# Issuing one attention tile and one output chunk ahead, and moving small elementwise steps between engines

## The chip, the cores and the metric

The kernel runs on one core of one Trainium2 chip. The metric is the device time in microseconds (us) of one execution; lower is better. TensorE is called PE here, VectorE DVE, ScalarE ACT, GpSimd POOL, and SyncE, whose queue issues nearly all the DMAs, SP. PEld is PE's weight load.

## The reference

One block of a network over 2048 tokens of width 448, in bf16. A vector c gives six modulation vectors (`silu(c) @ w_mod`). First half: layer norm, scale and shift, attention with 16 heads of width 28 in its linear form, projection by `wo`, gated residual. The feature map of a head is a softmax of `q @ w_phi` joined with a softmax of its negative (the same for k). Second half: layer norm, scale and shift, a gated MLP that mixes along the tokens, gated residual.

```python
# attention, per head: phi(u) = concat(softmax(u w_phi), softmax(-u w_phi))
kv  = phi(k)^T v                 # summed over all 2048 tokens
z   = sum over tokens of phi(k)
o   = (phi(q) kv) / (phi(q) z + 1e-6)
x   = x + ga * (o @ wo)
# gated MLP
zz  = gelu(h @ w_in)             # 448 -> 1792
z1, z2 = first 896, layernorm(last 896)
g   = w_sp @ z2 + b_sp           # 2048 x 2048 over the tokens
x   = x + gb * ((z1 * g) @ w_out)
```

## The kernel before, in words

The program is written for a planner. The Python code issues operations in some order, which counts as their priority; the planner sorts each engine's queue before the run, taking what is ready by its own reckoning, earlier-issued work first, and adds the semaphores. At run time every engine takes its queue strictly in order. Tiles of one tag share a fixed number of buffers (`bufs`), so an operation can also wait for a buffer.

Tokens are worked in 16 tiles of 128, and in four super-tiles of 512 tokens (four tiles each).

- **First stage (A1).** For each tile: k and v (lines 235, 236) in PSUM, `softmax_feats` (lines 196 to 209) on k, the sums over features and their reciprocal on DVE (239, 240), the scaled features `phik` on POOL (242), and the accumulation of `kvacc` on PE (249). `softmax_feats` takes the maximum and minimum of each head on DVE (200, 201), subtracts the maximum (203, DVE), forms minimum minus maximum, 16 numbers a token (204, DVE), forms the negated half from it (205, POOL), and takes the exponential on ACT (208).
- **Late setup.** `late_setup` (253) folds the gates into the weights: `g_rep` holds two gate rows on all partitions in float32 (266), `wo_s` is multiplied by the first (267, 268), the seven slices of `wout_s` by the second (270).
- **Second stage (A2).** For each super-tile `st`: `a2_q` on its four tiles (307: q, `softmax_feats`, a transposing DMA to `EqT`), then for each tile `il` first `a2_o` (316) and then, of the super-tile before, `a2_z2` (352) and a share of `a2_z1` (371). `a2_o` is the whole attention output of a tile: eight matmuls `num` (321), two reciprocals and two multiplies on DVE (326, 327), the sum `tt` and `rden` on POOL (329, 331), a reciprocal and the scaling `o_rot` on DVE (332, 334), a transposing DMA to `oT` (337), the projection with the residual `x1_ps` on PE (341, 342), layer norm through DVE and POOL (185 to 191), `xn2` on ACT (346) and four transposes into `tp` on PE (348). After the fourth tile ACT makes `h2T` from `tp` (396), on which `a2_z2` and `a2_z1` of this super-tile then work during the next. A fifth pass has only that last work. The two `num` halves share two PSUM banks, `x1_ps` and `z2_ps` share two (tag `xz`), `q_ps` and `z1_ps` share two (tag `qz`).
- **Last stage (B).** For each of four chunks of 512 tokens, and each of seven feature slices: 16 matmuls of 512 columns into `g_ps` (426), the bias on DVE (428), the product with `z1T` on POOL (429). When the seven are done, the chunk's four output tiles: seven matmuls over the slices (434), an eighth with the identity that adds the residual `x_sb` (435), a copy to bf16 on ACT (437), and the store (438). The weights of the next chunk are loaded by four transposing DMAs on SP (69).

Of the kernel before, what the change touches and what calls it, by code (L numbers as in the profile page):

```python
# [9 lines left out]
ALU = mybir.AluOpType  # L10
AX = mybir.AxisListType
BF = mybir.dt.bfloat16
F32 = mybir.dt.float32
PSUM = bass.MemoryType.PSUM

P = 128
D = 448
# [3 lines left out]
KC = 4  # L21
FH = 896
FC = 7
# [5 lines left out]
def kernel(  # L29
# [14 lines left out]
    dbg=None,  # L44
# [49 lines left out]
    g_rep = sl.tile([P, 2, D], F32, name="g_rep")  # L94
# [101 lines left out]
    def softmax_feats(pool, p_ps, tagp):  # L196
# [7 lines left out]
        nc.vector.tensor_tensor(out=mn[:], in0=mn[:], in1=mx[:], op=ALU.subtract)  # L204
# [48 lines left out]
    def late_setup():  # L253
# [13 lines left out]
        nc.vector.tensor_tensor(out=wo_s[:, 0:3, :], in0=wo_s[:, 0:3, :], in1=g_rep[:, 0:1, :].to_broadcast([P, 3, D]), op=ALU.mult)  # L267
        nc.vector.tensor_tensor(out=wo_s[0:64, 3, :], in0=wo_s[0:64, 3, :], in1=g_rep[0:64, 0, :], op=ALU.mult)
# [47 lines left out]
    def a2_o(i, il, EqT, tp):  # L316
# [20 lines left out]
        nc.sync.dma_start_transpose(out=oT[:], in_=o_pad[:])  # L337
        x1_ps = psA.tile([P, D], F32, name="x1_ps", tag="xz")
# [10 lines left out]
        if dbg is not None and "o" in dbg:  # L349
            nc.sync.dma_start(out=dbg["o"][i * P:(i + 1) * P, :], in_=o_pad[:, 0:D])  # L350
# [27 lines left out]
    prev = None  # L378
    for st in range(NST + 1):
# [3 lines left out]
        for il in range(4):  # L383
            if st < NST:
                a2_o(st * 4 + il, il, EqTs[il], tp)
            if prev is not None:
                pst, ph2T = prev
                a2_z2(pst * 4 + il, il, ph2T)
                for fc in range(*z1_split[il]):
                    a2_z1(pst, fc, ph2T)  # L390
            if st == 0:
                load_wsp_piece(wsp_tiles[0], 0, il) if False else None
        if st < NST:
            h2T = wk.tile([DC, KC, 512], BF, tag="h2T")
            for cc in range(KC):
                nc.scalar.activation(out=h2T[:, cc, :], in_=tp[:, cc, :], func=ACT.Identity,  # L396
                                     scale=colf[:, 12 + cc:13 + cc], bias=colf[:, 8 + cc:9 + cc])
            prev = (st, h2T)
    if dbg is not None:
# [14 lines left out]
    outv = out[0].rearrange("(n p) d -> n p d", p=P)  # L414
    for tcn in range(NTCH):
# [5 lines left out]
        wspT = wsp_tiles[tcn]  # L421
        tsl = slice(tcn * TCH, (tcn + 1) * TCH)
        for fc in range(FC):
            g_ps = psg.tile([P, TCH], F32, name="g_ps", tag="g")
            for sc_ in range(NT):
                nc.tensor.matmul(g_ps[:], lhsT=z2n[:, sc_, fc * P:(fc + 1) * P], rhs=wspT[:, sc_, :], start=(sc_ == 0), stop=(sc_ == NT - 1))  # L426
            gb_ = wk.tile([P, TCH], F32, tag="gb")
            nc.vector.tensor_tensor(out=gb_[:], in0=g_ps[:], in1=bsp[:, tsl], op=ALU.add)
            nc.gpsimd.tensor_tensor(out=z1T[:, fc, tsl], in0=gb_[:], in1=z1T[:, fc, tsl], op=ALU.mult)  # L429
        for tl in range(TCH // P):  # L430
            t = tcn * (TCH // P) + tl
            o_ps = pso.tile([P, D], F32, name="o_ps", tag="o")
            for fc in range(FC):
                nc.tensor.matmul(o_ps[:], lhsT=z1T[:, fc, t * P:(t + 1) * P], rhs=wout_s[:, fc, :], start=(fc == 0), stop=False)  # L434
            nc.tensor.matmul(o_ps[:], lhsT=ident[:], rhs=x_sb[:, t, :], start=False, stop=True)  # L435
            ot = wk.tile([P, D], BF, tag="ot")
            nc.scalar.copy(out=ot[:], in_=o_ps[:])  # L437
            nc.sync.dma_start(out=outv[t], in_=ot[:])
# [38 lines left out]
```

## Time and profile before

| what | value |
|---|---|
| median of 4 runs | 418.79 us (417.73 to 421.11) |
| the profiled execution | 417.73 us |
| its span in the profile | 415.9 us |
| mean granted PE clock | 0.852 of full speed |
| busy: PE, DVE, ACT, POOL | 318.1, 203.8, 152.6, 146.6 us |

The span is the part that the profiler saw; 1.8 us of the execution lie around it. Busy times are of the whole span, and the stages differ: PE is busy nearly all of the last stage, and no engine all of the others. Times in the rows further down are microseconds from the start of the span.

### The profile page before, as it was taken

How to read it: one execution, taken by the hardware profiler on the slowest of the kernel's cores; microseconds unless marked ns; L12 is line 12 of the kernel's file. 1: busy time of each engine (PE TensorE's matmuls, PEld its weight loads, DVE VectorE, ACT ScalarE, POOL GpSimd, SP SyncE). 2: the span in 40 equal slices, each digit the busy share in tenths (PEclk: the TensorE clock that was granted, in tenths of full speed). 3: DMA queues.
4: the chain of work that ended last, by engine and by line, in shares of the span. 5: the costliest groups of instructions: out<-in, count | busy, mean ns of one | idle time of the engine just before them, and what ended most of it. 6: DMA issues, size and time to landing. Idle time of an engine off the chain costs nothing.

```text
span 415.9 us, 4540 instructions
## 1 busy us (share of the span) xinstructions
PE 318.1 (76%) x1609; PEld 150.7 (36%) x1620; DVE 203.8 (49%) x471; ACT 152.6 (37%) x229; POOL 146.6 (35%) x198
## 2 busy tenths in 40 slices
PE   1668778544866869676686676499999999999995
PEld 1644334223322233323232232134444444444442
DVE  1478988874487865667456755235110110110110
ACT  1167827442130465559463955164002002002002
POOL 2035677772034543335223522112331331331331
PEclk9999868765556669966896699669999999999999
DMA  8999100000032241032203220000991008401001
GB/s 218 302 302 196 34 1 1 2 0 0 2 72 54 50 90 25 0 64 41 50 0 63 40 52 0 13 2 7 189 209 44 2 0 181 67 0 46 0 0 44
DMA packets 69071, 25.60 MB, mean 62 GB/s; under 512 B 59897, under 2 KB 68474, under 8 KB 69050
## 3 DMA queue, kind: packets, MB, share of 16 engines
q1 hardware_dynamic: 68082, 24.50, 28.2%
q10 hardware_dynamic: 968, 0.83, 0.9%
q8 instruction: 12, 0.20, 0.2%
q14 instruction: 9, 0.07, 0.1%
HBM read 8.81 MB, written 1.84 MB: 26 GB/s over the span
## 4 chain that ended last, share of the span: by engine, by line
PE 46%; DVE 19%; POOL 14%; ACT 8%; DMA 6%; issue 5%; SPq 1%; POOLq 0%; ACTq 0%; DVEq 0%
PE g_ps L426 23%; PE z_ps L357 4%; PE o_ps L434 4%; POOL phik L242 4%; PE x_ps L341 3%; POOL tt L329 3%; DVE sums L239 3%; PE z_ps L374 3%; DVE t L327 3%; POOL d L205 2%; DMA Wp<-in_A_wqkv_dram 2%; DMA wo_s<-in_A_wo_dram 2%; POOL rstd L189 2%; ACT xn L346 2%; ACT E_rot L208 2%
## 5 line engine op out<-in xcount | busy, mean ns | idle before, releaser
L426 PE MATMUL g_ps<-wspn,z2n 128*128 128x512 bf16 x328 | 72.6, 379 | 0.4
L426 PEld LDWEIGHTS <-z2n 128*128 128x128 bf16 x448 | 43.8, 98 | 53.6 <-issue 1.0
L437 ACT CAST ot<-o_ps 128x448 bf16<-128x448 f32 x16 | 8.5, 532 | 117.0 <-PE o_ps L435 115.4
L205 POOL TENSOR_TENSOR d<-mn,d 128x448 f32<-128x448 f32 x32 | 30.0, 942 | 37.5 <-DVE mn L204 37.4
L208 ACT ACTIVATE E_rot<-d 128x896 bf16<-128x896 f32 x32 | 30.1, 952 | 32.6 <-POOL d L205 32.6
L357 PE MATMUL z_ps<-win_sb,h2T 112*128 112x448 bf16 x128 | 33.9, 393 | 6.2 <-ACT z2g L359 5.1
L374 PE MATMUL z_ps<-h2T,win_sb 112*128 112x512 bf16 x112 | 35.3, 432 | 0.4 <-ACT h2T L396 0.4
L242 POOL TENSOR_TENSOR phik<-E_rot,sums 128x1024 bf16<-128x1024 bf16 x16 | 30.4, 1917 | 14.1 <-DVE sums L240 12.6
L310 PE MATMUL q_ps<-Wp,hT 112*128 112x448 bf16 x64 | 22.1, 483 | 11.0 <-DVE d L203 10.3
L341 PE MATMUL x_ps<-wo_s,oT 128*128 128x448 bf16 x64 | 23.9, 479 | 8.5 <-DMA oT<-o_rot 8.5
L434 PE MATMUL o_ps<-wout_s,z1T 128*128 128x448 bf16 x112 | 24.5, 353 | 3.1 <-POOL z1T L429 3.1
L188 POOL TENSOR_SCALAR rstd<-mv 128x1 f32<-128x1 f32 (+1 forms) x20 | 4.5, 223 | 63.0 <-DVE mv L186 55.2
L236 PE MATMUL v_ps<-Wp,hT 112*128 112x448 bf16 x64 | 22.6, 459 | 4.4 <-ACT vaug_rot L244 4.4
L321 PE MATMUL num<-KVbd,EqT 128*128 128x120 bf16 x128 | 15.6, 270 | 13.0 <-DVE t L327 9.3
L362 DVE BATCH_NORM_STATS2 stats<-z2g 128x6 f32<-128x448 bf16 x32 | 19.5, 621 | 11.7 <-ACT z2g L359 11.5
L329 POOL TENSOR_TENSOR tt<-t 128x464 f32<-128x464 f32 x16 | 16.4, 1024 | 24.6 <-DVE t L327 24.6
L426 PE MATMUL g_ps<-wsp,z2n 128*128 128x512 bf16 x109 | 24.2, 379 | 0.8 <-ACT z1T L375 0.7
L235 PE MATMUL k_ps<-Wp,hT 112*128 112x448 bf16 x64 | 21.7, 439 | 1.7 <-ACT hT L227 1.6
L357 PEld LDWEIGHTS <-h2T 112*128 112x128 bf16 x128 | 13.6, 107 | 22.0 <-issue 13.1
L359 ACT ACTIVATE z2g<-z_ps 128x448 bf16<-128x448 f32 x32 | 17.3, 544 | 9.0 <-PE z_ps L357 8.7
L239 DVE TENSOR_REDUCE sums<-E_rot 128x32 f32<-128x896 bf16 x16 | 16.9, 1067 | 7.5 <-ACT E_rot L208 7.5
L327 DVE TENSOR_TENSOR t<-num,rS 128x464 f32<-128x464 f32 x32 | 19.8, 628 | 0.3
(155 smaller groups left out, 496.0 us busy)
## 6 DMA issues: line engine op xcount, KB each, us to landing
x_sb<-in_A_x_dram SPq DMA_DIRECT2D x4, 448.0 KB, 5.7
out_dram<-ot SPq DMA_DIRECT2D x16, 112.0 KB, 1.7
win_sb<-in_B_w_in_dram SPq DMA_DIRECT2D x1, 1568.0 KB, 15.3
wmod_c<-in_w_mod_dram ACTq DMA_DIRECT2D x1, 784.0 KB
wmod_c<-in_w_mod_dram SPq DMA_DIRECT2D x1, 784.0 KB, 8.4
wmod_g<-in_w_mod_dram SPq DMA_DIRECT2D x2, 392.0 KB
wout_s<-in_B_w_out_dram SPq DMA_DIRECT2D x1, 784.0 KB, 16.7
bsp<-in_B_b_sp_dram SPq DMA_DIRECT2D x1, 512.0 KB
```

Of the source, the lines that this page charges most:

```text
L205: nc.gpsimd.tensor_tensor(out=d[:, :, 1, :], in0=mn[:].unsqueeze(2).to_broadcast([P, H, DH]), in1=d[:, :, 0, :], op=ALU.subtract)
L208: nc.scalar.activation(out=E[:, :, :, 0:DH], in_=d[:], func=ACT.Exp)
L236: nc.tensor.matmul(v_ps[:], lhsT=lhs, rhs=Wp[:, kc, 2 * D:3 * D], start=(kc == 0), stop=(kc == KC - 1))
L239: nc.vector.tensor_reduce(out=sums[:], in_=Ek[:, :, :, 0:DH], axis=AX.X, op=ALU.add)
L242: nc.gpsimd.tensor_tensor(out=phik[:], in0=Ek[:], in1=sums[:].unsqueeze(3).to_broadcast([P, H, 2, 32]), op=ALU.mult)
L327: nc.vector.tensor_tensor(out=t12[:, b], in0=numv[:, :, :, 0:29], in1=rS[:, b].unsqueeze(3).to_broadcast([P, 8, 2, 29]), op=ALU.mult)
L329: nc.gpsimd.tensor_tensor(out=tt[:], in0=t12[:, :, :, 0, :], in1=t12[:, :, :, 1, :], op=ALU.add)
L341: nc.tensor.matmul(x1_ps[:], lhsT=oT[0:kk, cc, :], rhs=wo_s[0:kk, cc, :], start=(cc == 0), stop=False)
L357: nc.tensor.matmul(z2_ps[:], lhsT=h2T[:, kc, il * P:(il + 1) * P], rhs=win_sb[:, kc, FH + hf * D:FH + (hf + 1) * D], start=(kc == 0), stop ...
L374: nc.tensor.matmul(z1_ps[:], lhsT=win_sb[:, kc, fc * P:(fc + 1) * P], rhs=h2T[:, kc, :], start=(kc == 0), stop=(kc == KC - 1))
L426: nc.tensor.matmul(g_ps[:], lhsT=z2n[:, sc_, fc * P:(fc + 1) * P], rhs=wspT[:, sc_, :], start=(sc_ == 0), stop=(sc_ == NT - 1))
L434: nc.tensor.matmul(o_ps[:], lhsT=z1T[:, fc, t * P:(t + 1) * P], rhs=wout_s[:, fc, :], start=(fc == 0), stop=False)
```

## The change

`a2_o` is cut in two after the `oT` transfer: `a2_o1` (from `num` to `oT`) and `a2_o2` (from the projection to the transposes). `a2_o1` of the next tile of the super-tile is now issued ahead of `a2_o2` of this tile and of the MLP work beside it. In the last stage the first feature slice of a chunk is issued ahead of the output tiles of the chunk before; the eighth matmul is gone, and the residual is added by DVE as it empties the PSUM bank, in place of ACT's copy. In `softmax_feats`, in both its uses, the small subtraction goes from DVE to POOL. `g_rep` is bf16, and `wo_s` is multiplied in four slices instead of two pieces.

```diff
-    g_rep = sl.tile([P, 2, D], F32, name="g_rep")
+    g_rep = sl.tile([P, 2, D], BF, name="g_rep")
...
-        nc.vector.tensor_tensor(out=mn[:], in0=mn[:], in1=mx[:], op=ALU.subtract)
+        nc.gpsimd.tensor_tensor(out=mn[:], in0=mn[:], in1=mx[:], op=ALU.subtract)
...
-        nc.vector.tensor_tensor(out=wo_s[:, 0:3, :], in0=wo_s[:, 0:3, :], in1=g_rep[:, 0:1, :].to_broadcast([P, 3, D]), op=ALU.mult)
-        nc.vector.tensor_tensor(out=wo_s[0:64, 3, :], in0=wo_s[0:64, 3, :], in1=g_rep[0:64, 0, :], op=ALU.mult)
+        for cc in range(KC):
+            kk = P if cc < 3 else D - 3 * P
+            nc.vector.tensor_tensor(out=wo_s[0:kk, cc, :], in0=wo_s[0:kk, cc, :], in1=g_rep[0:kk, 0, :], op=ALU.mult)
...
-    def a2_o(i, il, EqT, tp):
+    def a2_o1(i, EqT):
...
         nc.sync.dma_start_transpose(out=oT[:], in_=o_pad[:])
+        return oT
+
+    def a2_o2(i, il, oT, tp):
         x1_ps = psA.tile([P, D], F32, name="x1_ps", tag="xz")
...
+    def a2_g(il):
+        if prev is not None:
+            pst, ph2T = prev
+            a2_z2(pst * 4 + il, il, ph2T)
+            for fc in range(*z1_split[il]):
+                a2_z1(pst, fc, ph2T)
+
     for st in range(NST + 1):
         if st < NST:
             EqTs = [a2_q(st * 4 + il) for il in range(4)]
             tp = psA.tile([DC, KC, 512], BF, name="tp2", tag="tp", bufs=1)
-        for il in range(4):
-            if st < NST:
-                a2_o(st * 4 + il, il, EqTs[il], tp)
-            if prev is not None:
-                pst, ph2T = prev
-                a2_z2(pst * 4 + il, il, ph2T)
-                for fc in range(*z1_split[il]):
-                    a2_z1(pst, fc, ph2T)
...
+            oTs = [None] * 4
+            oTs[0] = a2_o1(st * 4, EqTs[0])
+            for il in range(4):
+                if il + 1 < 4:
+                    oTs[il + 1] = a2_o1(st * 4 + il + 1, EqTs[il + 1])
+                a2_o2(st * 4 + il, il, oTs[il], tp)
+                a2_g(il)
...
+        else:
+            for il in range(4):
+                a2_g(il)
...
+    def b_unit(tcn, fc):
+        wspT = wsp_tiles[tcn]
+        tsl = slice(tcn * TCH, (tcn + 1) * TCH)
+        g_ps = psg.tile([P, TCH], F32, name="g_ps", tag="g")
+        for sc_ in range(NT):
+            nc.tensor.matmul(g_ps[:], lhsT=z2n[:, sc_, fc * P:(fc + 1) * P], rhs=wspT[:, sc_, :], start=(sc_ == 0), stop=(sc_ == NT - 1))
+        gb_ = wk.tile([P, TCH], F32, tag="gb")
+        nc.vector.tensor_tensor(out=gb_[:], in0=g_ps[:], in1=bsp[:, tsl], op=ALU.add)
+        nc.gpsimd.tensor_tensor(out=z1T[:, fc, tsl], in0=gb_[:], in1=z1T[:, fc, tsl], op=ALU.mult)
+
+    def b_out(tcn):
+        for tl in range(TCH // P):
+            t = tcn * (TCH // P) + tl
+            o_ps = pso.tile([P, D], F32, name="o_ps", tag="o")
+            for fc in range(FC):
+                nc.tensor.matmul(o_ps[:], lhsT=z1T[:, fc, t * P:(t + 1) * P], rhs=wout_s[:, fc, :], start=(fc == 0), stop=(fc == FC - 1))
+            ot = wk.tile([P, D], BF, tag="ot")
+            nc.vector.tensor_tensor(out=ot[:], in0=o_ps[:], in1=x_sb[:, t, :], op=ALU.add)
+            nc.sync.dma_start(out=outv[t], in_=ot[:])
+
     for tcn in range(NTCH):
...
         for fc in range(FC):
-            g_ps = psg.tile([P, TCH], F32, name="g_ps", tag="g")
...
-            nc.tensor.matmul(o_ps[:], lhsT=ident[:], rhs=x_sb[:, t, :], start=False, stop=True)
-            ot = wk.tile([P, D], BF, tag="ot")
-            nc.scalar.copy(out=ot[:], in_=o_ps[:])
-            nc.sync.dma_start(out=outv[t], in_=ot[:])
+            b_unit(tcn, fc)
+            if fc == 0 and tcn > 0:
+                b_out(tcn - 1)
+    b_out(NTCH - 1)
```

## Rows read from the trace of the kernel before

**Rows 1.** Windows by stage: start:end, length, busy (instructions) per engine, PE clock, DMA.
```profile
49.00:99.00 50.00, 29.76 (x211) 15.26 (x209) 38.92 (x71) 24.55 (x37) 34.86 (x25) 0.73 0.00 1
117.00:288.00 171.00, 124.76 (x569) 53.10 (x570) 104.47 (x267) 93.67 (x137) 60.92 (x112) 0.78 0.20 37
288.00:415.90 127.90, 120.85 (x565) 55.71 (x573) 19.88 (x29) 8.52 (x16) 32.89 (x29) 1.00 0.32 64
```
**Rows 2.** Timeline of PE, second chunk's outputs: start, us, operation [idle before <-releaser].
```profile
343.00 1.49 PE L434 MATMUL o_ps<-wout_s,z1T 128*128 128x448 bf16 x7
...
345.25 0.36 PE L434 MATMUL o_ps<-wout_s,z1T 128*128 128x448 bf16 x1 [0.76 <-POOL z1T L429]
...
346.78 0.35 PE L435 MATMUL o_ps<-x_sb,ident 128*128 128x448 bf16 x1
```
**Rows 3.** Groups by line and shape: count | busy us, mean ns | idle before, releasers.
```profile
L437 ACT CAST ot<-o_ps 128x448 bf16<-128x448 f32 x16 | 8.5, 532 | 117.0 <-PE o_ps L435 115.4 <-DMA out_dram<-ot 1.7
L203 DVE TENSOR_TENSOR d<-q_ps,mx 128x448 f32<-128x448 f32 x16 | 9.7, 604 | 0.0
```
**Rows 4.** Timeline of SP's queue, same place as the second group.
```profile
343.20 4.84 SPq L69 DMA_TRANSPOSE wspn<-in_B_w_sp_dram  x2
348.13 1.01 SPq L438 DMA_DIRECT2D out_dram<-ot  x2
```
**Rows 5.** Timeline of PE, ends of the third and fourth super-tile.
```profile
208.17 0.35 PE L341 MATMUL x_ps<-wo_s,oT 128*128 128x448 bf16 x1
...
214.65 0.58 PE L321 MATMUL num<-KVbd,EqT 128*128 128x120 bf16 x8
...
223.38 1.78 PE L341 MATMUL x_ps<-wo_s,oT 128*128 128x448 bf16 x4
...
249.81 0.35 PE L341 MATMUL x_ps<-wo_s,oT 128*128 128x448 bf16 x1
...
256.99 0.58 PE L321 MATMUL num<-KVbd,EqT 128*128 128x120 bf16 x8
...
265.37 1.78 PE L341 MATMUL x_ps<-wo_s,oT 128*128 128x448 bf16 x4 [6.94 <-DMA oT<-o_rot]
```
**Rows 6.** Timeline of DVE, turn from the third to the fourth super-tile.
```profile
220.86 0.61 DVE L200 TENSOR_REDUCE mx<-q_ps 128x16 f32<-128x448 f32 x1
...
222.46 0.16 DVE L204 TENSOR_TENSOR mn<-mn,mx 128x16 f32<-128x16 f32 x1
222.54 0.61 DVE L200 TENSOR_REDUCE mx<-q_ps 128x16 f32<-128x448 f32 x1
...
231.14 1.19 DVE L327 TENSOR_TENSOR t<-num,rS 128x464 f32<-128x464 f32 x2
```
**Rows 7.** Timeline of DVE, then of PE, late setup; one group by shape.
```profile
111.40 3.84 DVE L270 TENSOR_TENSOR wout_s<-wout_s,g_rep 128x448 bf16<-128x448 bf16 x7 [1.68 <-ACT g_rep L266]
115.15 0.62 DVE L200 TENSOR_REDUCE mx<-q_ps 128x16 f32<-128x448 f32 x1
...
111.41 3.15 PE L310 MATMUL q_ps<-Wp,hT 112*128 112x448 bf16 x8 [0.62 <-ACT g_rep L266]
...
L368 DVE TENSOR_SCALAR z2n<-z2g,mv,rstd 128x896 bf16<-128x896 bf16 x16 | 8.2, 512 | 15.4 <-POOL rstd L367 15.4
```
**Rows 8.** Timeline of POOL, first stage; one row of DVE's; one group by shape.
```profile
63.33 1.85 POOL L205 TENSOR_TENSOR d<-mn,d 128x448 f32<-128x448 f32 x2
67.35 3.79 POOL L242 TENSOR_TENSOR phik<-E_rot,sums 128x1024 bf16<-128x1024 bf16 x2 [2.16 <-DVE sums L240]
71.10 1.84 POOL L205 TENSOR_TENSOR d<-mn,d 128x448 f32<-128x448 f32 x2
...
85.37 0.94 POOL L205 TENSOR_TENSOR d<-mn,d 128x448 f32<-128x448 f32 x1 [2.33 <-DVE mn L204]
...
91.84 0.94 POOL L205 TENSOR_TENSOR d<-mn,d 128x448 f32<-128x448 f32 x1 [0.45 <-DVE mn L204]
...
39.47 1.70 DVE L204 TENSOR_TENSOR mn<-mn,mx 128x16 f32<-128x16 f32 x1
...
L331 POOL TENSOR_SCALAR rden<-tt 128x16 f32<-128x16 f32 x16 | 5.1, 321 | 1.4
```

More of the change, by code (lines that the diff above doesn't have):

```diff
@@ L337, in a2_o @@
         nc.sync.dma_start_transpose(out=oT[:], in_=o_pad[:])
+        if dbg is not None and "o" in dbg:
+            nc.sync.dma_start(out=dbg["o"][i * P:(i + 1) * P, :], in_=o_pad[:, 0:D])
+        return oT
+    def a2_o2(i, il, oT, tp):
         x1_ps = psA.tile([P, D], F32, name="x1_ps", tag="xz")
@@ L348, in a2_o @@
             nc.tensor.transpose(tp[:, cc, il * P:(il + 1) * P], xn2[:, cc * DC:(cc + 1) * DC], ident[:])
-        if dbg is not None and "o" in dbg:
-            nc.sync.dma_start(out=dbg["o"][i * P:(i + 1) * P, :], in_=o_pad[:, 0:D])
     def a2_z2(i, il, h2T):
@@ L382 @@
             tp = psA.tile([DC, KC, 512], BF, name="tp2", tag="tp", bufs=1)
-        for il in range(4):
-            if st < NST:
-                a2_o(st * 4 + il, il, EqTs[il], tp)
-            if prev is not None:
-                pst, ph2T = prev
-                a2_z2(pst * 4 + il, il, ph2T)
-                for fc in range(*z1_split[il]):
-                    a2_z1(pst, fc, ph2T)
-            if st == 0:
-                load_wsp_piece(wsp_tiles[0], 0, il) if False else None
-        if st < NST:
+            oTs = [None] * 4
[5 more added lines that the diff above has]
+                a2_g(il)
             h2T = wk.tile([DC, KC, 512], BF, tag="h2T")
@@ L420 @@
             wsp_tiles.append(nxt)
-        wspT = wsp_tiles[tcn]
-        tsl = slice(tcn * TCH, (tcn + 1) * TCH)
         for fc in range(FC):
-            g_ps = psg.tile([P, TCH], F32, name="g_ps", tag="g")
[L425 to L434, printed above, removed]
-            nc.tensor.matmul(o_ps[:], lhsT=ident[:], rhs=x_sb[:, t, :], start=False, stop=True)
-            ot = wk.tile([P, D], BF, tag="ot")
-            nc.scalar.copy(out=ot[:], in_=o_ps[:])
-            nc.sync.dma_start(out=outv[t], in_=ot[:])
+            b_unit(tcn, fc)
+            if fc == 0 and tcn > 0:
+                b_out(tcn - 1)
+    b_out(NTCH - 1)
     pso.release()
```

## The prediction

> **What bounds the kernel now.** I read the windows by stage first, because a mean over the span hides that the stages have different limits [rows 1]. In the last stage PE is busy 120.85 of 127.9 us at a granted clock of 1.00, while DVE, ACT and POOL together work less than half of it: there only fewer matmuls or fewer stalls of PE buy time. In the second stage, 171 us, no engine is full: PE 124.76 at a clock of 0.78, so much of that is matmuls at the lower level, DVE 104.47, ACT 93.67, POOL 60.92. Such a stage is bound by chains of waits, so the order of the queues decides it. In the first stage POOL and DVE are the fullest, 34.86 and 38.92 of 50 us, neither full.
>
> Then I read the timelines where the edits land. In the last stage PE issues seven output matmuls at 343.00 and the next at 345.25, released by POOL [rows 2]: the output tile must wait for the bias and the product of the chunk's last slice. In the second stage PE issues the `num` matmuls of the fourth tile of a super-tile late, after the MLP work of the third, and then stands until the tile's `oT` has landed: 256.99 to 265.37 in the last turn, with 6.94 us of idle PE, and 214.65 to 223.38 in the turn before, where queries of the next super-tile fill part of it [rows 5]. These are what the change is aimed at; the sum goes part by part, against the profiled execution of 417.73 us (span 415.9, the rest around it), which is 1.06 us below the median of the four runs.
>
> **Last stage.** Removed: 16 matmuls with the identity. From the matmul at 345.25 to that at 346.78 are eight steps in 1.53 us, 0.19 each [rows 2], so 16 x 0.19 = 3.0 us, all on PE, which sets the end. Moved: the first slice of the next chunk ahead of a chunk's outputs. Seven steps should take 1.33 us, the trace has 2.25, so a stall of 0.92; it occurs four times, and for the last chunk nothing can be put in front, so 3 x 0.92 = 2.8 us. The cover is one slice of 16 matmuls of 512 columns, an estimated 16 x 0.19 x 512 / 448 = 3.5 us by the same step, against the 2.25 that pass now. If the planner took the outputs first, the 2.8 would be lost. The residual goes from ACT's copy of 0.532 us to a DVE add of a PSUM and an SBUF operand; the nearest row, a DVE subtraction of the same width from PSUM, takes 0.604 [rows 3]. DVE is busy 19.88 of 127.9 us [rows 1], so the 16 adds hide under PE except the last one: 0.07 us. Behind a blocked add on DVE stands the bias of the next slice, and PE has four banks for slices. The stores are also issued from a place where SP has just been handed the next chunk's transposing loads, 4.84 us for two of them [rows 4]; a store delayed by all four could hold the fourth add (three `ot` buffers) and the biases behind it for some 10 us at most, which four banks of 3.5 us each cover. I take nothing. Sum: 3.0 + 2.8 - 0.1 = 5.7 us.
>
> **Second stage.** Nothing is added or removed; `num` and everything up to `oT` of the next tile gets priority over the projection and MLP work of this one. Only the fourth tile is really late now, so only that counts. With priority over the third tile's projection it is issued no later than that projection's first matmul, at 249.81 in the last turn and 208.17 in the one before [rows 5]. From `num` to the fourth projection took 265.37 - 256.99 = 8.4 us and 223.38 - 214.65 = 8.7 us. So the projection could start at 249.81 + 8.4 = 258.2 instead of 265.37, 7.2 us earlier, and at 216.9 instead of 223.38, 6.5 us earlier. In the last turn nothing else stands between it and the last stage: 7.2 us. What is late next there is the MLP work of the last super-tile, which fills PE. In the two middle turns (the trace repeats the pattern) the next super-tile's softmax comes in: 1.68 us a tile on DVE (222.54 - 220.86, [rows 6]), 6.7 us for four, and the first `t` of the next super-tile waited on DVE until 231.14. That softmax has to be done in any order and competes with the earlier layer norm, so of 6.5 us I keep 4 a turn; the bounds are 0 and 6.5. The first super-tile has no MLP work beside it: nothing. SP gets the fourth `oT` transfer earlier, ahead of transfers of the next super-tile that aren't ready then. Sum: 7.2 + 2 x 4 = 15.2 us, bounds 7 and 20. A denser PE might also be granted its full clock for longer; I count nothing for it.
>
> **Late setup.** The seven `wout_s` products hold DVE from 111.40 to 115.15, 0.536 us each, and the first q softmax starts right behind them, though the eight matmuls of its first two tiles began at 111.41 and take 3.15 us, so the first of them was ready by about 113.0 [rows 7]. No row has a DVE product of two bf16 operands from SBUF. The upper bound of its cost is today's 0.536; the lower is half of the one-operand bf16 row of twice the width, 0.512 / 2 = 0.256 [rows 7]. I take a value near the lower end, 0.265, as that row shares memory and type: 7 x 0.27 = 1.9 us, just what the ready q allows. Bounds 0 and 2.0. The `wo_s` products, now four, lie in front of a wait for ACT's second `g_rep` and cost nothing.
>
> The Trainium skill (VectorE: DVE Perf Modes, the perf-mode tier table) has two results per cycle for a tensor_tensor of bf16 from SBUF and one for a float32 operand; by its figures an estimate is 1.8 us for the seven. That agrees with the value taken, which doesn't rest on it.
>
> **The small subtraction.** Off DVE: its slot in an undisturbed burst is 0.08 us (222.46 to 222.54, [rows 6]), though a call that met POOL's `phik` took 1.70 [rows 8]. On POOL: no row has it; the nearest, another 16-wide operation, takes 0.321 [rows 8]. It needs the maximum and minimum alone, so POOL can do it while DVE makes the first half of `d` (0.604, [rows 3]); POOL's queue behind it holds `d`, `phik` and the layer-norm steps. In the first stage the loop runs over POOL: two `d` at 63.33, two `phik` at 67.35, the next two `d` at 71.10, 7.77 us for two tiles [rows 8], of which DVE's slot of 0.08 is no part; so relieving DVE buys little, and POOL has 2.16 us idle in each round in which the step can sit. I take 0; below nothing is possible by a better order, above by the rivals.
>
> Sum: 5.7 + 15.2 + 1.9 = 22.8; 417.73 - 22.8 = 394.9, so 395 us.
>
> **Rivals.**
> First, the second stage keeps its order: the planner already takes what is ready, and it may place the fourth `num` where it did, for its operand or its banks. For it speaks that the other tiles' `num` already run ahead; against it, that the fourth waits for nothing in the trace when it is issued [rows 5]. Then 417.73 - 5.7 - 1.9 = 410.
>
> Second, the subtraction lands on POOL's part of the chain everywhere: 32 x (0.32 - 0.08) = 7.7 us, 394.9 + 7.7 = 403. For it: POOL's queue is in order and its loop sets the first stage; against it the 2.16 us of idle in each round. The Trainium skill (GPSIMD Engine Reference, Engine selection) advises against GpSimd for elementwise work, two-input operations being about twice as slow there as on VectorE; no row here has the same two-input operation on both.
>
> Third, the first stage falls into a shorter rhythm. At its end, with single tiles, `d` comes at 85.37 and two tiles later at 91.84, 3.24 us a tile against 7.77 / 2 = 3.89 [rows 8]. Taking the subtraction out of DVE's queue, where it stood behind the sums, favours that. For some ten tiles: 6.5 us, 388.
>
> Fourth, slower: POOL's queue becomes serial in the first stage, `d` and `phik` of one tile before the next tile's subtraction. From `d` to `phik` take 4.02 us (63.33 to 67.35), a `phik` 1.9, the subtraction 0.32: 6.24 a tile instead of 3.89 [rows 8], times 16 a loss of 38 us, 433. It decides from a loss of 22.8 / 16 = 1.4 us a tile, a spacing of 5.3. Against it: the planner paired tiles before, and nothing that it saw forbids it now.
>
> **How the numbers follow.** Forecast 0.58, with 387 to 401 of its own (the middle turns at either bound, setup, some clock); order unchanged 0.15; subtraction on the chain 0.12; shorter rhythm 0.10; serial POOL 0.05. The first and last ends of all but the serial case give 386 to 410. About 1% (4.2 us) is what a measurement here can tell from no change: below 414.6 lie all but the serial case and a small part of the first rival, should its setup and last-stage gains fail too. Faster 0.91, same 0.04, slower 0.05.
>
> **What would show it.** In the last stage: line 435 gone, and PE's wait for POOL at an output tile once, at the end, instead of four times. In the second: the fourth `num` ahead of the third projection, and the wait for `oT` of 6.94 us down to under 2. In late setup: the `wout_s` group at half its 3.84 us and the q softmax right behind. In the first stage: POOL's round still about 7.8 us for two tiles. The prediction is wrong if the fourth `num` stays behind the MLP work, if an earlier projection only moves the wait to the softmax of the next super-tile, or if POOL's round grows.

## The result and the profile after

The changed kernel takes 397.07 us (median of 11 runs, 392.95 to 402.31) against 419.27 us for the one before (16 runs): a ratio of 0.946, with a 95% interval of 0.942 to 0.949. Two of the eleven, at 401.72 and 402.31 us, ran in a slower state of the chip at a lower clock and are left out of the ratio. The forecast was 395. The profiled execution took 397.74 us, its span is 395.8, so between the two profiled executions lie 20.0 us, a little less than the 22.2 between the medians.

The windows by stage of the changed kernel, in the columns of [rows 1]; the last one is cut at 273.40 instead of 288.00:

```profile
49.00:99.00 50.00, 29.48 (x205) 14.41 (x204) 33.90 (x60) 25.35 (x37) 36.49 (x37) 0.76 0.00 1
117.00:273.40 156.40, 115.84 (x569) 50.65 (x567) 102.94 (x252) 89.08 (x133) 64.07 (x125) 0.85 0.22 41
273.40:395.80 122.40, 117.62 (x549) 54.66 (x559) 29.77 (x45) 0.00 (x0) 33.15 (x30) 1.00 0.32 67
```

The second stage does the same work in 14.6 us less by these windows, and no engine is full in it now either (PE 115.84 of 156.40 us); its order, its waits and its clock (0.85 for 0.78) differ. The last stage is shorter by 5.5 in this table (by 5.8 from its first matmul, 128.23 to 122.41), with ACT empty and DVE up by the 16 adds. Exactly, the last stage begins 14.3 us earlier. PE's first matmuls of it, as far as the view's window reaches, in the kernel before and in the changed one:

```profile
287.67 12.68 PE L426 MATMUL g_ps<-wsp,z2n 128*128 128x512 bf16 x56 [0.69 <-ACT z1T L375]
273.39 24.33 PE L432 MATMUL g_ps<-wsp,z2n 128*128 128x512 bf16 x109 [0.69 <-ACT z1T L379]
```

In what follows, the second stage is measured from the first q matmul to the first of these: 176.26 us before (111.41 to 287.67), 160.52 in the changed kernel (112.87 to 273.39).

PE at the seams of the last stage, in the timeline of the changed kernel:

```profile
301.01 5.46 PE L442 MATMUL o_ps<-wout_s,z1T 128*128 128x448 bf16 x28
306.52 24.12 PE L432 MATMUL g_ps<-wspn,z2n 128*128 128x512 bf16 x109
...
388.28 4.15 PE L442 MATMUL o_ps<-wout_s,z1T 128*128 128x448 bf16 x21 [0.83 <-POOL z1T L435]
```

Four output tiles now go through in one piece, 28 matmuls in 5.46 us, and slices follow with no gap, where [rows 2] show a stop after seven. The one wait for POOL left is that of the last chunk, at 388.28.

PE at the third super-tile's last projection and through the fourth (the stretch of [rows 5]); lines 321 and 341 are now 322 and 347:

```profile
209.56 1.02 PE L347 MATMUL x_ps<-wo_s,oT 128*128 128x448 bf16 x4
...
225.99 1.00 PE L322 MATMUL num<-KVbd,EqT 128*128 128x120 bf16 x8
...
234.24 1.71 PE L347 MATMUL x_ps<-wo_s,oT 128*128 128x448 bf16 x4
...
236.84 0.38 PE L322 MATMUL num<-KVbd,EqT 128*128 128x120 bf16 x4
...
246.50 1.02 PE L347 MATMUL x_ps<-wo_s,oT 128*128 128x448 bf16 x4
...
252.14 1.02 PE L347 MATMUL x_ps<-wo_s,oT 128*128 128x448 bf16 x4
```

The last `num` (236.84) stands ahead of the third projection (246.50), and the fourth follows that one by 5.64 us, where it was 15.56 (249.81 to 265.37, [rows 5]). Of all waits of PE the view by line has for `oT` (total, times, longest):

```profile
PE x_ps L347 <- DMA oT<-o_rot: 2.1, 4, 0.9
```

But compare the first projections. Those of the third and fourth super-tile in the kernel before, then that of the third in the changed one:

```profile
194.84 1.02 PE L341 MATMUL x_ps<-wo_s,oT 128*128 128x448 bf16 x4
...
237.94 1.62 PE L341 MATMUL x_ps<-wo_s,oT 128*128 128x448 bf16 x4
...
192.43 1.03 PE L347 MATMUL x_ps<-wo_s,oT 128*128 128x448 bf16 x4 [0.31 <-DMA oT<-o_rot]
```

Call the time from a super-tile's fourth projection to the next one's first the turn. In the kernel before, the fourth super-tile ran from 237.94 to 265.37, and the turn to it from 223.38 to 237.94. Now the super-tile takes 17.9 us (234.24 to 252.14) instead of 27.4, and the turn 24.7 us (209.56 to 234.24) instead of 14.6: most of what the third super-tile gains is given back at the turn behind it. Only behind the last super-tile is there no turn.

What DVE does in that turn, in the timeline of the changed kernel:

```profile
212.53 0.60 DVE L200 TENSOR_REDUCE mx<-q_ps 128x16 f32<-128x448 f32 x1
...
220.86 0.62 DVE L200 TENSOR_REDUCE mx<-q_ps 128x16 f32<-128x448 f32 x1 [0.76 <-POOL mn L204]
...
221.93 1.14 DVE L203 TENSOR_TENSOR d<-q_ps,mx 128x448 f32<-128x448 f32 x2
226.63 0.66 DVE L327 RECIPROCAL rS<-num 128x16 f32<-128x16 f32 x2 [3.56 <-PE num L322]
```

And SP's queue, in its own timeline:

```profile
220.87 9.18 SPq L314 DMA_TRANSPOSE EqT<-E_rot  x4
```

The softmaxes of the next super-tile's four tiles hold DVE from 212.53 to 223.07, mixed with layer norms; their transposes start at 220.87; DVE then stands 3.56 us for a `num` that comes of them. ACT is part of the delay: POOL had the first tile's `d` ready at 217.13, but ACT worked on `h2T` (2.79 us) and loaded a table (1.28 us) before it took that tile's exponential at 219.89.

### The profile page after: what moved, and what is told of

Read it like the earlier page. It is cut to its first block, busy times and chain, and to the rows that moved or that the text cites. A ratio compares the mean times of both kernels' runs of the same rounds, so it can differ in the third digit from the quotient of the medians.

```text
span 395.8 us, 4533 instructions
## 1 busy us (share of the span) xinstructions
PE 305.5 (77%) x1593; PEld 146.4 (37%) x1604; DVE 204.4 (52%) x457; ACT 139.5 (35%) x209; POOL 153.7 (39%) x230
## 4 chain that ended last, share of the span: by engine, by line
PE 38%; DVE 10%; POOL 6%; ACT 3%; issue 2%; POOLq 0%; ACTq 0%; DVEq 0%
PE g_ps L432 24%; PE o_ps L442 5%; PE z_ps L378 4%; PE z_ps L361 2%; POOL rstd L189 2%; DVE stats L366 2%; DVE z2n L372 2%; POOL rstd L371 2%; DVE stats L185 1%; ACT xn L352 1%; DVE t L328 1%; POOL tt L330 1%; PE num L322 1%; ACT z2g L363 1%; POOL rstd L370 1%
## 5 line engine op out<-in xcount | busy, mean ns | idle before, releaser
L378 PE MATMUL z_ps<-h2T,win_sb 112*128 112x512 bf16 x112 | 37.7, 453 | 2.8 <-DVE d L203 1.8
L242 POOL TENSOR_TENSOR phik<-E_rot,sums 128x1024 bf16<-128x1024 bf16 x16 | 30.5, 1917 | 14.4 <-DVE sums L240 11.3
L361 PE MATMUL z_ps<-win_sb,h2T 112*128 112x448 bf16 x128 | 30.6, 362 | 2.9 <-ACT z2g L363 1.7
L311 PE MATMUL q_ps<-Wp,hT 112*128 112x448 bf16 x64 | 19.7, 438 | 8.6 <-DVE d L203 7.8
L235 PE MATMUL k_ps<-Wp,hT 112*128 112x448 bf16 x64 | 22.8, 438 | 3.1 <-ACT hT L227 1.6
L366 DVE BATCH_NORM_STATS2 stats<-z2g 128x6 f32<-128x448 bf16 x32 | 19.3, 612 | 9.8 <-ACT z2g L363 9.6
L322 PE MATMUL num<-KVbd,EqT 128*128 128x120 bf16 x128 | 15.2, 263 | 10.7 <-DVE t L328 8.0
L239 DVE TENSOR_REDUCE sums<-E_rot 128x32 f32<-128x896 bf16 x16 | 17.1, 1076 | 12.1 <-ACT E_rot L208 11.9
L442 PE MATMUL o_ps<-wout_s,z1T 128*128 128x448 bf16 x112 | 22.0, 353 | 0.8 <-POOL z1T L435 0.8
L347 PE MATMUL x_ps<-wo_s,oT 128*128 128x448 bf16 x64 | 19.7, 406 | 2.1 <-DMA oT<-o_rot 2.1
L249 PE MATMUL kvacc<-vaug_rot,phik 128*128 128x58 bf16 x128 | 7.9, 213 | 15.1 <-POOL phik L242 15.1
L361 PEld LDWEIGHTS <-h2T 112*128 112x128 bf16 x128 | 12.5, 99 | 16.3 <-issue 5.9
```

The costliest lines, as they stand in the source:

```text
L235: nc.tensor.matmul(k_ps[:], lhsT=lhs, rhs=Wp[:, kc, D:2 * D], start=(kc == 0), stop=(kc == KC - 1))
L242: nc.gpsimd.tensor_tensor(out=phik[:], in0=Ek[:], in1=sums[:].unsqueeze(3).to_broadcast([P, H, 2, 32]), op=ALU.mult)
L361: nc.tensor.matmul(z2_ps[:], lhsT=h2T[:, kc, il * P:(il + 1) * P], rhs=win_sb[:, kc, FH + hf * D:FH + (hf + 1) * D], start=(kc == 0), stop ...
L366: nc.vector.bn_stats(out=stats[:, hf, :], in_=z2g[:, hf, :])
L378: nc.tensor.matmul(z1_ps[:], lhsT=win_sb[:, kc, fc * P:(fc + 1) * P], rhs=h2T[:, kc, :], start=(kc == 0), stop=(kc == KC - 1))
```

## The experiments

All ratios are to the kernel before, run beside each experiment on the same chip; the time of before was 418.3 to 419.9 us there.

**Everything except the subtraction.** The changed kernel with one line put back:

```diff
-        nc.gpsimd.tensor_tensor(out=mn[:], in0=mn[:], in1=mx[:], op=ALU.subtract)
+        nc.vector.tensor_tensor(out=mn[:], in0=mn[:], in1=mx[:], op=ALU.subtract)
```

> The changed kernel with the small subtraction back on DVE. Theory: on POOL it lengthens POOL's round in the first stage (7.77 us for two tiles before, 8.47 to 8.73 after) and gives nothing in the second, so this runs 3 to 4 us faster than the changed kernel, 393 us, with the last accumulation of the first stage back at about 98.5 us (102.4 in the changed kernel) and an unchanged second stage. Rival: freeing DVE in the softmax bursts is part of what shortened the second stage; then the first stage gains 4 us and the second loses as much, 397 us or more.

Measured: 395.44 us, 0.945 (0.939 to 0.951); span 394.3, the last `kvacc` at 99.91 against 102.39 with the step on POOL, the first q matmul at 112.78 against 112.87. The last `kvacc` comes 2.5 us later with the step on POOL, and the first q matmul does not. Neither theory had that: the one expected 3 to 4 us less, the other a longer second stage. On top of the rest the step is worth nothing that shows in the time.

It does show at the turn. PE's fourth projection of the third super-tile and first of the fourth in this run:

```profile
211.17 1.02 PE L347 MATMUL x_ps<-wo_s,oT 128*128 128x448 bf16 x4
...
230.87 1.02 PE L347 MATMUL x_ps<-wo_s,oT 128*128 128x448 bf16 x4
```

That is 19.7 us, against 24.7 in the changed kernel, and the fourth super-tile begins 3.4 us earlier than there; from there to the last stage this run takes 1.9 us more (41.0 against 39.2).

**The subtraction alone**, in the kernel before.

```diff
-        nc.vector.tensor_tensor(out=mn[:], in0=mn[:], in1=mx[:], op=ALU.subtract)
+        nc.gpsimd.tensor_tensor(out=mn[:], in0=mn[:], in1=mx[:], op=ALU.subtract)
```

> The kernel before with the small subtraction on POOL and nothing else. Theory: slower by 3 to 4 us (422 to 423), all of it in the first stage, whose last accumulation moves from 98.5 to about 102.4 us. Rival: the longer rounds came from the planner's order for the whole changed program; alone it changes nothing (419), or the relief of DVE shows and it is faster (415).

Measured: 411.81 us, 0.986 (0.978 to 0.993), under 2% but clear of no change: the theory had a loss, the rival a smaller gain (415 us), from the relief of DVE. The last `kvacc` comes 3.2 us later (101.69 against 98.53), the first q matmul 0.7 earlier (110.68; the eight gate matmuls right before it took 1.67 us at a granted clock of 1.00 here, 3.14 at 0.50 in the changed kernel), and the second stage is 7.6 shorter (168.65 against 176.26). PE's timeline at the fourth tile of the fourth super-tile:

```profile
244.50 0.27 PE L321 MATMUL num<-KVbd,EqT 128*128 128x120 bf16 x2
...
245.76 0.37 PE L321 MATMUL num<-KVbd,EqT 128*128 128x120 bf16 x4
...
250.07 0.27 PE L321 MATMUL num<-KVbd,EqT 128*128 128x120 bf16 x2
...
257.48 1.79 PE L341 MATMUL x_ps<-wo_s,oT 128*128 128x448 bf16 x4 [4.30 <-DMA oT<-o_rot]
```

The planner, with one step on another engine, sorts PE's queue otherwise: the eight `num` that stood at 256.99 in one piece [rows 5] are issued in three, 6.9 to 12.5 us earlier by the two spans' times, and the wait for `oT` at the last projection is 4.30 instead of 6.94. (The super-tile as a whole lies 4.9 earlier.) The fourth projection follows the third by 9.76 us (247.72 to 257.48) instead of 15.56; the split makes that 5.64. So the subtraction alone removes a part of the same delay that the split removes, and with the split in place the time shows nothing left of it to remove. It is a gain of order and not of fewer waits for `oT`: there are nine of these now, 13.1 us in all, for three and 8.5 before.

**The subtraction on POOL for the queries alone**, to part the first stage from the second.

```diff
-        nc.vector.tensor_tensor(out=mn[:], in0=mn[:], in1=mx[:], op=ALU.subtract)
+        (nc.vector if tagp == "k" else nc.gpsimd).tensor_tensor(out=mn[:], in0=mn[:], in1=mx[:], op=ALU.subtract)
```

> The kernel before with the small subtraction on POOL for the queries alone (second stage), on DVE for the keys. Alone for both, the change made the kernel 6.5 us faster, against expectation. Theory: that gain is one of order: with the subtraction out of DVE's queue the planner puts part of the fourth tile's num in front of the MLP work of the third; it is all in the second stage, so 411 to 412 us here. Rival: it comes from the first stage or from the PE clock carried over from it, which the keys' subtraction changed; then 418 here.

Measured: 413.67 us, 0.984 (0.980 to 0.988), the second stage 171.71, the longest wait for `oT` 4.3 us as in the run above, and the last `kvacc` at 99.53. The gain is the second stage's; but this run has 4.5 of the 7.6 us there. The other 3.1 are not the order's: in the second stage PE, DVE, ACT and POOL take the same instructions in the same order in both traces. The clock differs a little (0.79 in the run above, 0.78 here); that it explains all 3.1 is not shown.

**The attention split alone**: `a2_o1`, `a2_o2`, `a2_g` and the loop over the super-tiles of the changed kernel, in the kernel before:

```diff
-                a2_o(st * 4 + il, il, EqTs[il], tp)
+                if il + 1 < 4:
+                    oTs[il + 1] = a2_o1(st * 4 + il + 1, EqTs[il + 1])
+                a2_o2(st * 4 + il, il, oTs[il], tp)
+                a2_g(il)
```

> The kernel before with the attention output cut in two and issued one tile ahead, nothing else. Theory: the second stage (first query matmul at 111.4, first matmul of the last stage at 287.7 us) shortens by 13 to 15 us as it did in the changed kernel, 404 to 406 us in all, with under 2 us of PE waiting for the last oT. Rival: the change needs the freed DVE slots of the small subtraction; then 8 us or less, 411 us.

Measured: 403.77 us, 0.964 (0.959 to 0.970). The second stage is 161.85 us, 14.4 less than before; the last stage 128.22, unchanged.

**Only the fourth tile ahead**, otherwise the order of before:

```diff
+                if il < 3:
+                    oTs[il] = a2_o1(st * 4 + il, EqTs[il])
+                if il == 2:
+                    oTs[3] = a2_o1(st * 4 + 3, EqTs[3])
+                a2_o2(st * 4 + il, il, oTs[il], tp)
+                a2_g(il)
```

> The kernel before with the attention output cut in two, but only the fourth tile's first half issued ahead of the third tile's projection; the other tiles in the order of before. Theory: only the fourth num was late, so the second stage is as short as with all tiles ahead (about 162 us from the first query matmul to the first matmul of the last stage, 404 us in all). Rival: the lead of every tile counts; then about half, 411 us.

Measured: 404.17 us, 0.963 (0.960 to 0.966), second stage 161.77: as the whole split, within 0.1 us. The other tiles had no late `num`, as the prediction had it; the planner's queue for PE is the same in both runs but for one MLP matmul. The first projections of the third and fourth super-tile and the first matmul of the last stage:

```profile
194.83 1.03 PE L346 MATMUL x_ps<-wo_s,oT 128*128 128x448 bf16 x4
...
231.31 1.37 PE L346 MATMUL x_ps<-wo_s,oT 128*128 128x448 bf16 x4
...
273.19 24.33 PE L437 MATMUL g_ps<-wsp,z2n 128*128 128x512 bf16 x112 [0.69 <-ACT z1T L378]
```

This run's first q matmul comes at 111.42, as in the kernel before, so its times compare directly: the third super-tile begins no earlier, the fourth 6.6 us earlier, the last stage 14.5. A higher clock of PE is not what shortens the stage: it was 0.79 here and 0.80 in the whole split, and with the subtraction back on DVE the stage took 159.11 us at 0.80, in the changed kernel 160.52 at 0.84.

**The gates in bf16 alone**: `g_rep` and the products of `wo_s` as in the changed kernel.

```diff
-    g_rep = sl.tile([P, 2, D], F32, name="g_rep")
+    g_rep = sl.tile([P, 2, D], BF, name="g_rep")
```

> The kernel before with the gate rows in bf16 and wo_s in four slices. Theory: the seven wout_s products take about 2.2 us instead of 3.84, the first query softmax starts 1.6 to 1.9 us earlier behind the first query matmul, and so does all that follows: 416.5 us. Rival: the start of the second stage is held by something else (PE's query matmuls at the lower clock, the first EqT transfer), and the time stays at 418.

Measured: 414.37 us, 0.987 (0.983 to 0.990), more than expected. DVE at the late setup in this run:

```profile
112.36 2.20 DVE L271 TENSOR_TENSOR wout_s<-wout_s,g_rep 128x448 bf16<-128x448 bf16 x7 [2.48 <-ACT g_rep L266]
114.48 0.62 DVE L200 TENSOR_REDUCE mx<-q_ps 128x16 f32<-128x448 f32 x1
```

From the first product to the first softmax pass 2.12 us, 0.30 a product, against 3.75 and 0.536 [rows 7]; the softmax begins 2.10 behind the first q matmul (112.38) instead of 3.74. That is 1.6 us shown. The second stage is 3.5 shorter (172.73), at a clock of 0.78 for 0.77, its queues in the order of before on all four engines, and the medians lie 5.5 apart. What the rest is, isn't settled; the next run says how far executions with this order can differ.

**The output part alone**: `b_unit` and `b_out` of the changed kernel.

```diff
-        for tl in range(TCH // P):
...
+            b_unit(tcn, fc)
+            if fc == 0 and tcn > 0:
+                b_out(tcn - 1)
+    b_out(NTCH - 1)
```

> The kernel before with the last stage of the changed one: the first slice of a chunk ahead of the outputs of the chunk before, the residual on DVE. Theory: 5.7 us less, 413.5 us, all of it behind the first matmul of the last stage. Rival: the gain in the last stage comes partly from a PE clock that is granted earlier after a shorter second stage; then 3 us or less, 416.

Measured: 412.75 us, 0.985 (0.979 to 0.991); the last stage 122.49 us, 5.7 less. The second stage, which this edit doesn't touch, took 2.3 us longer in the profiled run, at a lower clock. Its window by stage, from the first q matmul to the first matmul of the last stage:

```profile
111.20:289.71 178.51, 130.77 (x577) 55.61 (x576) 110.62 (x278) 93.78 (x137) 60.55 (x110) 0.75 0.19 36
```

The kernel before has 176.26 us for it, at 0.77 (111.41 to 287.67), with the same order on all four engines. So 2 us of this stage can come and go from one execution to another; the longer one had the lower clock.

**The residual on DVE alone**: no eighth matmul, the add on DVE in place of ACT's copy, the order of before.

```diff
-            nc.tensor.matmul(o_ps[:], lhsT=ident[:], rhs=x_sb[:, t, :], start=False, stop=True)
...
-            nc.scalar.copy(out=ot[:], in_=o_ps[:])
+            nc.vector.tensor_tensor(out=ot[:], in0=o_ps[:], in1=x_sb[:, t, :], op=ALU.add)
```

> The kernel before with the residual added by DVE in place of the eighth matmul and ACT's copy, in the order of before. Theory: 16 x 0.19 = 3.0 us less, 415.3 us, with PE's four waits for POOL at a chunk's first output tile still there. Rival: the waits grow by what the matmuls gave (the next chunk's slices do not start sooner), and nothing is gained; or most of the 5.5 us of the whole last-stage change come from here, 413.

Measured: 414.97 us, 0.989 (0.986 to 0.993); the last stage 125.25 us, 3.0 less, and PE still waits for POOL four times in it, 3.1 us in total. The first of them in PE's timeline:

```profile
312.22 1.49 PE L434 MATMUL o_ps<-wout_s,z1T 128*128 128x448 bf16 x7
314.47 1.88 PE L434 MATMUL o_ps<-wout_s,z1T 128*128 128x448 bf16 x9 [0.76 <-POOL z1T L429]
```

With the slice ahead as well, 122.49 above: that is the other 2.8.

**The subtraction on POOL for the keys alone**, in the changed kernel.

```diff
-        nc.gpsimd.tensor_tensor(out=mn[:], in0=mn[:], in1=mx[:], op=ALU.subtract)
+        (nc.gpsimd if tagp == "k" else nc.vector).tensor_tensor(out=mn[:], in0=mn[:], in1=mx[:], op=ALU.subtract)
```

> The changed kernel with the small subtraction on POOL for the keys (first stage) and on DVE for the queries. Theory: on top of the other parts the subtraction brings nothing: the fourth num is already early, so its side effect on the order of the second stage is gone, and the first stage's longer rounds end in the late setup, which waits for the folded query weights; 395 to 397 us, the first query matmul within 1 us of the 112.8 us of both other versions. Rival: the first stage's longer rounds do reach the second stage: 398 to 399.

Measured: 395.56 us, 0.944 (0.939 to 0.949), span 393.9. With the other two forms (0.946 on POOL throughout, 0.945 on DVE throughout) all intervals overlap: where the split is in, the step's engine makes no difference to the time that is measured. The second stage, with the queues in the order of the run with the step on DVE throughout, takes 159.51 us (159.11 there), and its last turn 19.3 us (211.23 to 230.52). So the turn of 24.7 goes with the queries' step on POOL.

**The next softmax spread over the tiles**, to try whether it is what is late at the turn: the changed kernel with the subtraction on DVE, and each tile's query work for the next super-tile issued behind a tile of this one.

```diff
-            EqTs = [a2_q(st * 4 + il) for il in range(4)]
+            EqTs = nxtq if st else [a2_q(il) for il in range(4)]
+            nxtq = []
...
                 a2_o2(st * 4 + il, il, oTs[il], tp)
+                if st + 1 < NST:
+                    nxtq.append(a2_q((st + 1) * 4 + il))
                 a2_g(il)
```

> The changed kernel with the small subtraction on DVE and with the queries and softmax of the next super-tile's tile il issued right behind this super-tile's projection of tile il, ahead of the MLP work. Theory: in the changed kernel the gain inside a super-tile is given back at the two middle turns (from the fourth projection to the first of the next super-tile 14.6 us before, 24.7 after), since the four softmaxes come as a burst; spread, the turn falls to about 14 us, 2 x 8 to 10 us less in the second stage, but each tile's exponential among gelus costs more table loads on ACT (1.28 us each), so 382 to 388 us. Rival: the turn is bound by ACT and the transposing DMAs, or the spread work only takes the slots of the layer norms; then 394 to 400.

Measured: 392.40 us, 0.937 (0.935 to 0.939), between the theory's range and the rival's. The kernel to compare with is the first experiment, which has the subtraction on DVE too: 395.44 us, so a gain of 3.0. The third super-tile's first and last projection and the turn to the fourth, in PE's timeline:

```profile
188.22 1.81 PE L347 MATMUL x_ps<-wo_s,oT 128*128 128x448 bf16 x4
...
216.85 1.02 PE L347 MATMUL x_ps<-wo_s,oT 128*128 128x448 bf16 x4
...
222.35 1.02 PE L347 MATMUL x_ps<-wo_s,oT 128*128 128x448 bf16 x4
```

The turn is down from 19.7 us in that experiment to 5.5, but the third super-tile takes 28.6 us (188.22 to 216.85) instead of 16.3. The softmax competes inside the super-tile instead of behind it. ACT also changes its table more often in the second stage, 15 loads of 1.28 us for exponentials and gelus instead of 11.

**The next four softmaxes in one piece, ahead of the last tile's projection**: as above, with these lines in place of the appending ones:

```diff
+                if il == 3 and st + 1 < NST:
+                    nxtq = [a2_q((st + 1) * 4 + j) for j in range(4)]
                 a2_o2(st * 4 + il, il, oTs[il], tp)
                 a2_g(il)
```

> As spread_q, but the four query tiles of the next super-tile are issued together, ahead of the fourth projection of this one. Theory: half of the burst is hidden behind the fourth tile's MLP work, few table loads more: 388 to 391 us. Rival: the burst only delays the fourth projection by what it gains later: 394 to 396.

Measured: 391.75 us, 0.935 (0.931 to 0.939): the lowest median, not to be told from the spread form, 0.8 us above the expected range. The interval is clear of the changed kernel's (0.942 to 0.949) and just touches that of the first experiment (0.939 to 0.951), from which it differs by this move alone. DVE at the same turn, its first and last softmax step:

```profile
208.97 0.62 DVE L200 TENSOR_REDUCE mx<-q_ps 128x16 f32<-128x448 f32 x1
...
215.08 0.61 DVE L203 TENSOR_TENSOR d<-q_ps,mx 128x448 f32<-128x448 f32 x1
```

And PE there:

```profile
208.90 1.02 PE L347 MATMUL x_ps<-wo_s,oT 128*128 128x448 bf16 x4
...
225.32 1.78 PE L347 MATMUL x_ps<-wo_s,oT 128*128 128x448 bf16 x4 [0.30 <-DMA oT<-o_rot]
...
246.60 1.03 PE L347 MATMUL x_ps<-wo_s,oT 128*128 128x448 bf16 x4
```

DVE's part of the four softmaxes takes 6.7 us in one piece (208.97 to 215.69). Against the first experiment, the next super-tile's first projection comes 5.5 us earlier (225.32 for 230.87); inside the fourth super-tile 2.6 of these are lost again (21.3 us instead of 18.7), and the second stage is 4.0 us shorter (155.14 for 159.11). So the next super-tile's softmax is what is late at the turn. Which part of it, DVE's steps, ACT's exponentials and table loads or the transposes, is not parted: they move together.

## Why the prediction was right, step by step

The sum of 22.8 us stands against 22.2 between the medians and 20.0 between the two profiled executions. In these, the first q matmul comes 1.5 us later than before, the way from there to the last stage is 15.7 shorter (late setup and second stage, 17.1 predicted), and the last stage 5.8. By the signs that the prediction named for itself, two of those for its being wrong came true in part: POOL's round grew (8.46 us for 7.77), and at the two middle turns the earlier projection mostly moved the wait to the next super-tile's softmax. That the total still came out is in part luck, since misses within the second stage cancel.

**Last stage: right, term by term.** 3.0 predicted for the 16 matmuls, 3.0 measured with the residual alone; 2.8 for three stalls, 2.8 measured between the two runs of this part. The DVE add takes 0.62 us where ACT's copy took 0.532 [rows 3]:

```profile
302.54 0.62 DVE L444 TENSOR_TENSOR ot<-o_ps,x_sb 128x448 bf16<-128x448 f32 x1 [0.56 <-PE o_ps L442]
```

The delayed store came as described too. Among DVE's waits of the changed kernel stands one for an `ot` buffer (total, times, longest):

```profile
DVE ot L444 <- DMA out_dram<-ot: 5.5, 1, 5.5
```

Over PE lies nothing of it: its only waits in this stage are 0.83 for POOL at the end and 0.69 at the first matmul.

**Second stage: the sum was right, its division wrong.** 15.2 predicted; 14.4 measured with the split alone. The step that failed is the two middle turns, taken at 4 us each, between bounds of 0 and 6.5. Read the first projections of the super-tiles against before: the second super-tile's is 1.9 us earlier (154.56 for 156.46), the third's 2.4 (192.43 for 194.84), the fourth's 3.7 (234.24 for 237.94). So the turns brought 0.5 and 1.3. The prediction itself named the cause, the softmax of the next super-tile; it priced four tiles at 6.7 us of DVE as if in one piece. They took 10.5 (212.53 to 223.07), mixed with this super-tile's layer norms, one of them behind POOL, and their four transposes another 9.18 on SP's queue behind the first of them. The run with the softmax ahead bears it out.

With the split alone the terms fit better. In the run with the fourth tile alone the turns bring 0 and 6.6 us, the two ends of the stated bounds, and the rest to the last stage 7.9 for the 7.2 predicted; why the first of the two turns gives nothing there is open. The turn to the fourth super-tile takes 19.2 to 19.7 us in the four kernels with the split, no further reordering and the queries' subtraction on DVE, and 24.7 in the changed kernel. So a part of what was lost at this turn belongs to the small subtraction, which the prediction took at 0; the total doesn't show it, because the changed kernel's last part gains more.

The last turn was mis-sized the other way: 7.2 predicted, 9.5 measured from first to last projection of the fourth super-tile, and 10.6 to the start of the last stage (14.3 gained there, less the 3.7 before). The bound "no later than the third projection" was too careful: the last half of `num` goes right behind the first, at 236.84, and then nothing of its own holds the fourth projection; ahead of it in PE's queue stand the third tile's MLP work and its transposes, which wait 1.68 us for ACT's `xn2`. That only the fourth tile counts is shown by the run with that tile alone.

**Late setup: right, 1.6 for 1.9.** A product takes 0.30, not the 0.265 that was taken, and the softmax follows at once. The estimate of 1.8 us for seven from the Trainium skill (VectorE: DVE Perf Modes, the perf-mode tier table) is 0.3 below the measured 2.12 (the table's 1224 ns for 2048 elements gives an estimate of 1.87); that bf16 operands double the rate, the trace nearly agrees with: 0.536 to 0.30, a factor of 1.8.

**The small subtraction: 0 in sum, for reasons other than the two given.** The prediction had POOL's round of 7.77 us unchanged, because the step would sit in 2.16 us of idle. It doesn't. POOL in the first stage of the changed kernel:

```profile
56.86 0.94 POOL L205 TENSOR_TENSOR d<-mn,d 128x448 f32<-128x448 f32 x1
57.76 0.22 POOL L204 TENSOR_TENSOR mn<-mn,mx 128x16 f32<-128x16 f32 x1
58.06 0.94 POOL L205 TENSOR_TENSOR d<-mn,d 128x448 f32<-128x448 f32 x1
...
61.58 3.79 POOL L242 TENSOR_TENSOR phik<-E_rot,sums 128x1024 bf16<-128x1024 bf16 x2 [2.11 <-DVE sums L240]
65.32 0.94 POOL L205 TENSOR_TENSOR d<-mn,d 128x448 f32<-128x448 f32 x1
```

A slot is 0.30 (57.76 to 58.06), the round 8.46 (56.86 to 65.32), and the idle time ahead of `phik` is still 2.11. It was no slack: it is the way from the second `d` over the exponential and the sums back to `phik`, and it moves along with `d`. A step inside a loop of dependences lengthens it, also where its engine has idle time. That is the second rival's mechanism, in the first stage: the last `kvacc` comes 2.5 us later than with the step on DVE. (From the first k matmul to the last `kvacc` take 73.2 to 73.9 us in the three runs with the keys' step on POOL, 70.0 to 72.1 in the ten others.) It costs nothing further on that shows. PE's last `kvacc` and first q matmul, in the changed kernel, then in the first experiment, with the step on DVE:

```profile
102.39 0.57 PE L249 MATMUL kvacc<-vaug_rot,phik 128*128 128x58 bf16 x8 [0.43 <-POOL phik L242]
...
112.87 3.15 PE L311 MATMUL q_ps<-Wp,hT 112*128 112x448 bf16 x8 [0.62 <-ACT g_rep L266]
...
99.91 0.57 PE L249 MATMUL kvacc<-vaug_rot,phik 128*128 128x58 bf16 x8 [0.66 <-POOL phik L242]
...
112.78 2.77 PE L311 MATMUL q_ps<-Wp,hT 112*128 112x448 bf16 x7 [0.62 <-ACT g_rep L266]
```

The way from the one to the other is 10.5 us with the step on POOL and 12.9 with it on DVE. In between lies the folding of the query weights and the gates. Where the last `kvacc` is late, the queue has 10 of the 16 folding matmuls (`pf`, line 166) ahead of it, otherwise four. The work was there to fill the wait; the prediction didn't count on it.

The Trainium skill (GPSIMD Engine Reference, Engine selection) advises against GpSimd for two-input elementwise work; the trace agrees, with slots of 0.30 on POOL and 0.08 on DVE [rows 6], but here it decided nothing in the total.

**The other rivals.** The second stage didn't keep its order (410). No shorter rhythm came (388), and no serial one (433): the first stage stays in pairs until 74 us, at 8.4 to 8.7 us a round.

**The parts aren't additive.** Alone they gave 6.5 (subtraction), 14.5 (split), 5.5 (gates) and 5.5 us (output), 32 in sum, together 22. The overlap is in the second stage: the subtraction and the split shorten the same delay of the fourth projection, and with the split in, the subtraction gives nothing more. The gates' 5.5 is the other suspect, since 1.6 of it is accounted for. On top of the split they are worth 2.3 to 2.7 us: with the second stage's queues in the same order, it takes 161.85 us with the split alone, 159.11 and 159.51 in the two kernels that have the gates in bf16 too.

## What to carry to other kernels

When a stage is bound by waits, price a reordering by what comes late next, and count that work as it will really run (mixed with its neighbours, its transfers behind it), not as an undisturbed burst; then look at the seam behind it, where a gain inside a block may be given back. An idle gap inside a loop of dependences is no slack for one more step. And where a planner sorts the queues, a single moved step can gain or lose more through the order than by its own cost, so test it both alone and on top of the rest before it is kept.

## What the runs showed of the hardware that was not expected

The second stage with the same instructions in the same order on every engine ran 176.26 us at a granted clock of 0.77 in one execution, 176.26 at 0.76 in another and 178.51 at 0.75 in a third. A difference of 2 us in one execution of a stage like this says nothing by itself.

A tiny operation on DVE took eleven times its usual time beside POOL. In the first stage of the changed kernel, DVE's timeline:

```profile
46.75 1.76 DVE L191 SCALAR_TENSOR_TENSOR nmr<-mv,rstd 128x4 f32<-128x4 f32 x1
```

And POOL's:

```profile
44.70 3.79 POOL L242 TENSOR_TENSOR phik<-E_rot,sums 128x1024 bf16<-128x1024 bf16 x2 [2.32 <-DVE sums L240]
```

It ends when POOL's second `phik` does, at 48.5; the median of this line's 20 operations, of one or four columns, is 0.159. The subtraction that took 1.70 before [rows 8] has two operands from SBUF too. The thirteen traces together have 125 steps of these two lines (191, and 204 on DVE) that begin while one of POOL's big instructions (`phik`, `tt` or `d`) has at least 0.2 us to run, and all 125 end within 0.04 us behind that instruction. DVE steps that read one SBUF tensor keep their time beside POOL: 79 reciprocals of `sums` took 0.33 to 0.35 us each. So here a DVE step with two SBUF operands stood until the POOL instruction beside it was done. No run was made to test this by itself, and what the two engines share for it the traces don't show.
